# Gated feed-forward on one core: the second difference of the activations moved ahead of the first transient sum on VectorE, and the first difference's cast and lower part moved into the value's pass

## The chip, the cores and the metric

The kernel runs on one core of a Trainium2 chip. The metric is device time in microseconds (us) of one execution. Before the change three runs gave 2883.59, 2885.57 and 2885.86 us, so the median is 2885.57 us. The names of the engines are those of the profile: PE is TensorE (PEld its weight loads), DVE is VectorE, ACT is ScalarE, POOL is GpSimd, SP is SyncE, which here issues the DMAs.

## The reference

```python
# x is (8, 3008, 256); w_r, w_i are (256, 256); the feed-forward is 256 -> 1536 -> 256
X = np.fft.rfft(x, axis=1)
Yr = Xr @ w_r - Xi @ w_i + b_r
Yi = Xr @ w_i + Xi @ w_r + b_i
Yr = np.sign(Yr) * np.maximum(np.abs(Yr) - 0.01, 0.0)      # and Yi
y = np.fft.irfft(Y, n=3008, axis=1).reshape(24064, 256)
g = y @ w_gate
out = (g * (1 / (1 + np.exp(-g))) * (y @ w_val)) @ w_out
```

A Fourier layer with a soft threshold is followed by a gated feed-forward over 24064 tokens. Everything is float32.

## The kernel before

The kernel has two stages. `transform` does the Fourier layer, and in the trace it lasts about 680 us. `gated_ffn` does the rest, some 2200 us, and the change lies in it alone.

**Products.** A float32 operand is split into an upper part (its cast to fp32r) and a lower part (what the cast leaves). A product of two split operands is three matmuls that accumulate: weight-low times data-high, high times high, and high times low (`product`, L513, the matmul is on L516). Matrices are 2 by 2 blocks, and a 2 by 2 product is done with seven products in place of eight, by sums and differences of blocks.

**Blocks, pairs and halves.** The tokens come in 24 blocks. A block has two halves of 512 tokens (384 in the last two blocks), which are one side of the 2 by 2. Inside a block `q` runs over the six pairs of 128-wide slices of the hidden dimension (1536 = 6 x 2 x 128). Each `q` has two passes of `gate_or_value`: the gate (n = 0), which ends in a Silu, and the value (n = 1), which multiplies onto it. A pass has the seven up products of its weights, here called u1 to u7 (`up(bank, 1..7)`), in the order u1, u5, u6, u2, u7, u3, u4. Each product has its three matmuls.

**Down products.** While the gate and the value of one `q` are computed, the seven down products d1 to d7 of the pair before (`last`) are worked in between: d1, d3 and d2 in the gate, d6, d4, d7 and d5 in the value. So one `q` has 21 products, 63 matmuls, in this order on PE:

gate: u1, u5, d1, u6, d3, u2, u7, (inverse), u3, d2, u4; value: u1, u5, d6, u6, d4, u2, d7, u7, u3, d5, u4.

The piece "inverse" (L706) belongs to the last sequence of the Fourier layer: eight short matmuls in the gate of q = 2 of blocks 1 to 16.

**What d1 to d7 need.** The activations of a pair are four blocks H11, H12, H22 and H21 in `hidden`. VectorE makes four differences of them in `more` (`diff`, L527): T1 = H12 - H11, T3 = H22 - H12, T2 = H22 - T1, T4 = H21 - T2. Each of H11, H22, H21, T1, T3, T2, T4 is split: `upper` (L532) is the cast on ACT, `lower` (L536) the subtraction on POOL. d1 reads H11, d3 H22, d2 H21, d5 T1, d7 T3, d4 T4 and d6 T2. The differences all are done in the gate of the next pair, T1 and T3 at its start.

**PSUM.** There are eight banks. b1, b2 and b3 serve the up products. `spare` collects d1, then d1 + d6, then d1 + d6 + d7: after each, VectorE adds it to one of three running `sums` (`add`, L557, or a copy, L555, at q = 0), and must have read it before the next of the three writes it. Four banks hold totals over `q`. In each pass, ACT copies u1 from b1 to b3 (L623) and u5 from b2 to `m5` (L631); u6 is added onto b3 by PE, VectorE adds `m5` and b3 (L643), u7 is added onto b3, VectorE adds again (L666; in the gate the sum goes back to `m5`, which the Silu of H22 reads), then u4 is added onto b3. So u6 has to wait for the copy L623, u7 for the read on L643, and u4 for the read on L666.

**Order.** The four engines run in the order of the program, which is written out by hand (`tc.manual_schedule`); nothing reorders it. Besides the work above, ACT and POOL prepare the next block's `x` parts in the value passes: in q = 2 three sums on POOL (L502), in q = 3 one sum and two parts, in q = 4 two parts, in q = 5 three parts (a part is a cast on ACT, L510, and a subtraction on POOL, L511). When a block is complete, VectorE makes its outputs (`result`, L567) in the passes of the next block's q = 0 and q = 1.

Of the kernel before, what the change touches and what calls it, by code (L numbers as in the profile page):

```python
# [113 lines left out]
def f32(ap):  # L114
    return ap.bitcast(F32)
# [347 lines left out]
def gated_ffn(ctx, tc, front, ring, ps_, co, wdn, wup_d, xt_d, d2, out):  # L463

    nc = tc.nc
    v, g, act = nc.vector, nc.gpsimd, nc.scalar
# [9 lines left out]
    def load_unit(k):  # L476
        if k >= len(BLOCKS) * len(units):
            return
        held[k] = ring.tile([P, 2, 7, P], F32R, name="wup")
        nc.sync.dma_start(f32(held[k].rearrange("p i n a -> p i (n a)")), wup_d[units[k % len(units)]])  # L480
# [32 lines left out]
    def product(o, weights, parts, start, stop):  # L513

        for i, (w, x) in enumerate(((1, 0), (0, 0), (0, 1))):
            nc.tensor.matmul(o, lhsT=weights[w], rhs=parts[x], start=start and i == 0, stop=stop and i == 2, skip_group_check=True)  # L516


    H11, H12, H22, H21, T1, T3, T2, T4 = range(8)
    RIGHT = {1: H11, 3: H22, 2: H21, 5: T1, 7: T3, 4: T4, 6: T2}  # L520

    def at(i, h):
        return hidden[:, i, :h] if i < 4 else more[:, i - 4, :h]

    def diff(pair, o, a, b):
        h = pair["h"]
        v.tensor_tensor(at(o, h), at(a, h), at(b, h), op=ALU.subtract)  # L527

    def upper(pair, i):
        h = pair["h"]  # L530
        pair[i] = sbr.tile([P, 2, T], F32R, name="h_parts", bufs=8)
        act.copy(pair[i][:, 0, :h], at(i, h))  # L532

    def lower(eng, pair, i):
        h = pair["h"]
        eng.tensor_tensor(pair[i][:, 1, :h], at(i, h), f32(pair[i][:, 0, :h]), op=ALU.subtract)  # L536

    def down(pair, n_):

        h, q = pair["h"], pair["q"]  # L540
        weights = [part[:, q, A_AT[n_], :] for part in wdn]
        parts = [pair[RIGHT[n_]][:, x, :h] for x in range(2)]
        if n_ in total:
            product(total[n_][:, :h], weights, parts, q == 0, q == NQ - 1)
        else:
            product(spare[:, :h], weights, parts, n_ == 1, True)
# [4 lines left out]
    def add(pair, n_):  # L551
        h = pair["h"]
        o = sums[:, SUM_AT[n_], :h]
        if pair["q"] == 0:
            v.tensor_copy(o, spare[:, :h])  # L555
        else:
            v.tensor_tensor(o, o, spare[:, :h], op=ALU.add)  # L557

    def result(pair):

        h, blk = pair["h"], pair["blk"]
        o = {}

        def plus(c, j, n_, onto=None):
            if onto is not None:
                o[c, j] = sb.tile([P, T], F32, name="o", bufs=4)[:, :h]
            v.tensor_tensor(o[c, j], o[c, j] if onto is None else sums[:, onto, :h], total[n_][:, :h], op=ALU.add)  # L567

        def store(c, j):
            s = BLOCKS[blk][0] + (h if j == 1 else 0)  # L570
            nc.sync.dma_start(out[:, c - 1, s : s + h], o[c, j])

        plus(1, 1, 2, 0)
        store(1, 1)
        yield "after d2"
        plus(1, 2, 3, 1)
        yield "after d6"
        plus(2, 1, 4, 2)
        store(2, 1)
        yield "after d7"  # L580
        plus(1, 2, 5)
        store(1, 2)
        plus(2, 2, 5, 2)
        store(2, 2)
        yield "after d5"
# [3 lines left out]
    def step(name):  # L589

        if ends:
            assert next(ends["now"]) == name
            if name == "after d5":
                ends.clear()

    def gate_or_value(pair, last, n, k, extra):

        blk, q, h = pair["blk"], pair["q"], pair["h"]
        x = xs[blk]
        load_unit(k + RING - 1)  # L600
        m5 = hidden[:, 4 + n, :h]
        first = last is not None and last["q"] == 0
        closing = last is not None and last["q"] == NQ - 1

        def up(bank, n_, start):
            weights = [held[k][:, i, A_AT[n_], :] for i in range(2)]
            product(bank[:, :h], weights, [x[n_][:, i, :h] for i in range(2)], start, True)

        def done(after):
            for fn in extra.get(after, ()):  # L610
                fn()

        def take(i, src):

            if n == 0:
                act.activation(at(i, h), src, AF.Silu)  # L616
            else:
                v.tensor_tensor(at(i, h), at(i, h), src, op=ALU.mult)  # L618

        gate = n == 0 and last  # L620
        value = n == 1 and last
        up(b1, 1, True)
        act.copy(b3[:, :h], b1[:, :h])  # L623
        done(1)
        if gate:
            diff(last, T1, H12, H11)
            diff(last, T3, H22, H12)
        if value and first:
            step("after d5")
        up(b2, 5, True)  # L630
        act.copy(m5, b2[:, :h])  # L631
        done(5)
        if gate:
            upper(last, H21)
            lower(g, last, H21)
            upper(last, T3)
            lower(g, last, T3)
            down(last, 1)
        if value:
            down(last, 6)  # L640
            add(last, 6)
        up(b3, 6, False)
        v.tensor_tensor(b2[:, :h], m5, b3[:, :h], op=ALU.add)  # L643
        done(6)
        if gate:
            add(last, 1)
            down(last, 3)
            diff(last, T2, H22, T1)
        if value:
            if closing:  # L650
                step("after d6")
            down(last, 4)
        up(b1, 2, False)
        take(H11, b1[:, :h])
        if n:
            upper(pair, H11)
            lower(g, pair, H11)
        if gate:
            upper(last, T2)
            lower(g, last, T2)  # L660
        if value:
            down(last, 7)
            add(last, 7)
        up(b3, 7, False)
        last_sum = b1[:, :h] if n else m5
        v.tensor_tensor(last_sum, m5, b3[:, :h], op=ALU.add)  # L666
        if gate:
            diff(last, T4, H21, T2)
            if q == 2 and blk in pieces:
                inverse(pieces[blk])  # L670
        up(b2, 3, False)
        take(H22, last_sum)
        take(H12, b2[:, :h])
        if n:
            upper(pair, H22)
            lower(g, pair, H22)
        if gate:
            upper(last, T4)
            lower(g, last, T4)
            upper(last, T1)  # L680
            lower(g, last, T1)
            if first:
                step("after d7")
            down(last, 2)
            if closing:
                ends["now"] = result(last)
                step("after d2")
        if value:
            down(last, 5)
        up(b3, 4, False)  # L690
        take(H21, b3[:, :h])
# [11 lines left out]
    def inverse(u):  # L703
        for cc in range(2):
            for i in range(2):
                nc.tensor.matmul(  # L706
                    b1[:, cc * 188 + i * 94 : cc * 188 + (i + 1) * 94],
                    lhsT=part["z"][:, i * C + cc * P : i * C + (cc + 1) * P],
                    rhs=part["w"][:, i * 94 : (i + 1) * 94],
                    start=cc == 0 and i == 0,  # L710
                    stop=True,
                    skip_group_check=True,
                )
        xt = sbr.tile([P, 2, 188], F32, name="xt2")
        act.copy(xt.rearrange("p a b -> p (a b)"), b1[:, :376])
        nc.sync.dma_start(xt_d[B - 1][:, :, u * 188 : (u + 1) * 188], xt)
# [31 lines left out]
    last = None  # L748
    k = 0
    with tc.manual_schedule(engines={nc.tensor.engine, nc.vector.engine, nc.scalar.engine, nc.gpsimd.engine}):  # L750
        for blk, (_, h) in enumerate(BLOCKS):
            for q in range(NQ):
# [4 lines left out]
                last = pair  # L757
# [61 lines left out]
```

## Time and profile before

| | before |
|---|---|
| median of 3 runs | 2885.57 us |
| profiled execution, its time | 2883.66 us |
| its span, first to last instruction | 2881.9 us |
| mean granted TensorE clock | 0.990 |
| busy PE, PEld | 2734.9 us (95%), 2193.2 us (76%) |
| busy DVE, ACT, POOL | 2136.6 us (74%), 1721.8 us (60%), 1967.8 us (68%) |
| u and d matmuls (L516) | 9072 = 144 pairs x 63 |

In rows of the timeline the first number is the start in us from the span's start, the second how long the instructions of the row took, then engine, line, operation and tiles (written <- read), and how many instructions in a row were put together (x9). A bracket at the end gives the idle time of the engine ahead of the row and what ended it. A matmul's end is modelled and consecutive ones overlap, so the pace of PE is read from the starts.

### The profile page before, as it was taken

The numbers are of one execution on the slowest core, as the hardware profiler recorded it, in microseconds if no ns is written. First come the engines' busy times: TensorE is split into PE (matmuls) and PEld (weight loads), VectorE is DVE, ScalarE is ACT, GpSimd is POOL, SyncE is SP. The second block draws the span as 40 slices with busy tenths as digits, with TensorE's granted clock in tenths as the row PEclk, the third lists the DMA queues.
The fourth block names the chain that finished last, engine by engine and source line by source line (L and its number), as shares of the span: only waits on it lengthen the run. The fifth ranks groups of instructions, "written<-read, shape, count | busy, mean of one in ns | idle before, by whom it ended". The sixth has DMA issues, their size and how long they took to land. (4 is left out here: it accounts for less than half of the span.)

```text
span 2881.9 us, 39671 instructions
## 1 busy us (share of the span) xinstructions
PE 2734.9 (95%) x13173; PEld 2193.2 (76%) x13173; DVE 2136.6 (74%) x2916; ACT 1721.8 (60%) x3280; POOL 1967.8 (68%) x1574
## 2 busy tenths in 40 slices
PE   8989998899999999999999999999999999999998
PEld 5777787787777777777777777777777777777797
DVE  3766777875777777777777777777777777777777
ACT  5666666666565556556565556555565566555554
POOL 1555455564777778777777778777777777777775
PEclk9999999999999999999999999999999999999999
DMA  8788987664434444444434444444444443444442
GB/s 249 257 272 290 305 281 244 214 225 150 143 133 152 161 145 138 145 154 151 146 133 152 161 143 140 145 154 149 146 136 147 153 143 135 139 148 142 142 168 96
DMA packets 180124, 491.88 MB, mean 171 GB/s; under 512 B 17264, under 2 KB 89584, under 8 KB 179824
## 3 DMA queue, kind: packets, MB, share of 16 engines
q1 hardware_dynamic: 179920, 489.35, 51.4%
q8 instruction: 105, 1.72, 0.2%
q14 instruction: 99, 0.81, 0.1%
HBM read 378.65 MB, written 110.62 MB: 170 GB/s over the span
## 5 line engine op out<-in xcount | busy, mean ns | idle before, releaser
L516 PE MATMUL bank<-x_parts,wup 128*128 128x512 f32 (+1 forms) x6048 | 1551.3, 391 | 67.6 <-ACT bank L623 38.7
L516 PEld LDWEIGHTS bank<-x_parts,wup 128*128 128x128 f32 x6048 | 1108.9, 188 | 382.1 <-ACT bank L623 95.7
L536 POOL TENSOR_TENSOR h_parts<-more,h_parts 128x512 fp32r<-128x512 f32 (+1 forms) x573 | 769.5, 1354 | 191.1 <-ACT h_parts L532 185.9
L536 POOL TENSOR_TENSOR h_parts<-hidden,h_parts 128x512 fp32r<-128x512 f32 (+1 forms) x432 | 548.2, 1274 | 367.6 <-ACT h_parts L532 334.0
L516 PE MATMUL bank<-h_parts,wdn_hi 128*128 128x512 f32 (+1 forms) x2016 | 614.4, 386 | 0.9 <-POOL h_parts L536 0.9
L532 ACT CAST h_parts<-hidden 128x512 fp32r<-128x512 f32 (+1 forms) x432 | 264.9, 613 | 500.2 <-DVE hidden L618 500.2
L557 DVE TENSOR_TENSOR sums<-sums,bank 128x512 f32<-128x512 f32 (+1 forms) x360 | 242.7, 674 | 295.3 <-PE bank L516 295.3
L516 PEld LDWEIGHTS bank<-h_parts,wdn_hi 128*128 128x128 f32 x2016 | 378.2, 188 | 76.2 <-POOL h_parts L536 2.0
L618 DVE TENSOR_TENSOR hidden<-hidden,bank 128x512 f32<-128x512 f32 (+1 forms) x576 | 375.8, 674 | 79.8 <-PE bank L516 70.8
L532 ACT CAST h_parts<-more 128x512 fp32r<-128x512 f32 (+1 forms) x576 | 336.6, 610 | 158.3 <-DVE more L527 147.6
L516 PE MATMUL bank<-h_parts,wdn_lo 128*128 128x512 f32 (+1 forms) x1008 | 389.5, 386 | 4.2 <-DVE sums L557 4.2
L527 DVE TENSOR_TENSOR more<-hidden,more 128x512 f32<-128x512 f32 (+1 forms) x288 | 328.9, 1142 | 0.0
L616 ACT ACTIVATE hidden<-bank 128x512 f32<-128x512 f32 (+1 forms) x432 | 252.1, 584 | 126.0 <-PE bank L516 125.4
L643 DVE TENSOR_TENSOR bank<-hidden,bank 128x512 f32<-128x512 f32 (+1 forms) x288 | 197.3, 685 | 122.7 <-PE bank L516 91.5
L527 DVE TENSOR_TENSOR more<-hidden 128x512 f32<-128x512 f32 (+1 forms) x288 | 282.0, 1017 | 0.0
L623 ACT COPY bank<-bank 128x512 f32<-128x512 f32 (+1 forms) x288 | 161.6, 561 | 108.6 <-DVE hidden L618 103.9
L351 POOL TENSOR_TENSOR t<-t,y 128x512 f32<-128x512 f32 x96 | 132.9, 1384 | 136.2 <-DVE y L350 136.2
L516 PEld LDWEIGHTS bank<-h_parts,wdn_lo 128*128 128x128 f32 x1008 | 189.6, 188 | 41.7 <-issue 4.5
L511 POOL TENSOR_TENSOR x_parts<-xf,x_parts 128x512 fp32r<-128x512 f32 (+1 forms) x168 | 209.4, 1274 | 6.1 <-ACT x_parts L510 3.9
L316 POOL TENSOR_TENSOR f<-f 128x256 f32<-128x256 f32 x96 | 84.5, 880 | 149.1 <-ACT f L315 146.1
L631 ACT COPY hidden<-bank 128x512 f32<-128x512 f32 (+1 forms) x288 | 167.5, 582 | 1.8
L349 ACT COPY t<-mixb 64x256 f32<-64x256 f32 x384 | 140.6, 366 | 29.7 <-PE mixb L337 19.1
(94 smaller groups left out, 3278.3 us busy)
## 6 DMA issues: line engine op xcount, KB each, us to landing
wup<-wup_d SPq DMA_DIRECT2D x288, 896.0 KB, 4.6
d<-a SPq DMA_DIRECT2D x128, 192.0 KB, 4.3
a_in<-d SPq DMA_DIRECT2D x96, 256.0 KB, 4.4
out<-o SPq DMA_DIRECT2D x88, 256.0 KB, 6.4
scratch<-xp SPq DMA_DIRECT2D x116, 192.0 KB, 4.7
d<-z SPq DMA_DIRECT2D x84, 256.0 KB, 3.8
z_in<-d SPq DMA_DIRECT2D x56, 384.0 KB, 5.1
xt_d<-xt SPq DMA_DIRECT2D x56, 376.0 KB, 4.2
```

What stands on the lines that cost most here:

```text
L349: nc.scalar.copy(t[64 * half : 64 * half + 64, k * C : (k + 1) * C], mixb[64 * k : 64 * k + 64, half * C : (half + 1) * C])
L511: g.tensor_tensor(part[:, 1, :h], src, f32(part[:, 0, :h]), op=ALU.subtract)
L516: nc.tensor.matmul(o, lhsT=weights[w], rhs=parts[x], start=start and i == 0, stop=stop and i == 2, skip_group_check=True)
L527: v.tensor_tensor(at(o, h), at(a, h), at(b, h), op=ALU.subtract)
L532: act.copy(pair[i][:, 0, :h], at(i, h))
L536: eng.tensor_tensor(pair[i][:, 1, :h], at(i, h), f32(pair[i][:, 0, :h]), op=ALU.subtract)
L557: v.tensor_tensor(o, o, spare[:, :h], op=ALU.add)
L616: act.activation(at(i, h), src, AF.Silu)
L618: v.tensor_tensor(at(i, h), at(i, h), src, op=ALU.mult)
L623: act.copy(b3[:, :h], b1[:, :h])
L631: act.copy(m5, b2[:, :h])
L643: v.tensor_tensor(b2[:, :h], m5, b3[:, :h], op=ALU.add)
```

## The change

In the gate, VectorE's order behind L643 was: add of d1 (`add(last, 1)`), difference T2, L666, difference T4. It becomes: difference T2, L666, difference T4, add of d1. The cast of T1 on ACT and its lower part on POOL, which stood at the end of the gate behind those of T4, go to the value's pass, behind the copy of u5 (and behind the `x` parts that are placed after u1 and u5) and ahead of d6. Nothing is added or removed. The end of the program behind the last block is as before.

```diff
         if value:
+            upper(last, T1)
+            lower(g, last, T1)
             down(last, 6)
             add(last, 6)
         up(b3, 6, False)
         v.tensor_tensor(b2[:, :h], m5, b3[:, :h], op=ALU.add)
         done(6)
         if gate:
-            add(last, 1)
+            diff(last, T2, H22, T1)
             down(last, 3)
-            diff(last, T2, H22, T1)
...
         v.tensor_tensor(last_sum, m5, b3[:, :h], op=ALU.add)
         if gate:
             diff(last, T4, H21, T2)
+            add(last, 1)
             if q == 2 and blk in pieces:
                 inverse(pieces[blk])
...
         if gate:
             upper(last, T4)
             lower(g, last, T4)
-            upper(last, T1)
-            lower(g, last, T1)
             if first:
                 step("after d7")
```

## The prediction

> **What bounds the kernel now.** I read the stretch of the feed-forward first, in the view by windows (its columns are busy us and instructions of PE, PEld, DVE, ACT and POOL, then the granted clock, DMA share and GB/s), and then the row of the up matmuls in the view by lines.
>
> ```profile
> 681.00:2719.00 2038.00, 1976.10 (x8426) 1551.82 (x8426) 1556.93 (x2077) 1202.10 (x2151) 1526.22 (x1167) 1.00 0.43 145
> ```
>
> ```profile
> L516 PE MATMUL bank<-x_parts,wup 128*128 128x512 f32 (+1 forms) x6048 | 1551.3, 391 | 67.6 <-ACT bank L623 38.7 <-DVE hidden L666 28.4 <-POOL x_parts L511 0.2
> ```
>
> PE is busy 97% of the stretch at a granted clock of 1.00, no other engine over 77%. PE is the bound, and only what makes PE wait can pay. The row of the up matmuls names two causes beyond a trace of others: ACT's copy of u1 to b3 (L623) and VectorE's second sum (L666). The times there (38.7 and 28.4 us) are too small, since a matmul's end is modelled; the starts tell more. PE in q = 4 of block 12:
>
> ```profile
> 1857.74 2.20 PE L516 MATMUL bank<-x_parts,wup 128*128 128x512 f32 x9
> 1859.78 0.39 PE L516 MATMUL bank<-h_parts,wdn_lo 128*128 128x512 f32 x1
> 1860.00 0.61 PE L516 MATMUL bank<-h_parts,wdn_hi 128*128 128x512 f32 x2
> 1860.83 2.35 PE L516 MATMUL bank<-x_parts,wup 128*128 128x512 f32 x9 [0.21 <-DVE hidden L666]
> 1863.02 0.39 PE L516 MATMUL bank<-h_parts,wdn_lo 128*128 128x512 f32 x1
> 1863.25 0.61 PE L516 MATMUL bank<-h_parts,wdn_hi 128*128 128x512 f32 x2
> 1864.17 0.96 PE L516 MATMUL bank<-x_parts,wup 128*128 128x512 f32 x3 [0.30 <-ACT bank L623]
> 1864.97 0.40 PE L516 MATMUL bank<-h_parts,wdn_lo 128*128 128x512 f32 x1
> ```
>
> Nine matmuls without a wait take 1859.78 - 1857.74 = 2.04 us, so a matmul 0.227 and a product 0.68 us; the 63 of a pair would need 14.28 us. I count from d1 of this gate, three products ahead of the first row: 0 = 1855.70. Without waits the slots begin: u2 2.04, u7 2.72, u3 3.40, d2 4.08, u4 4.76, the value's u1 5.44, u5 6.12, d6 6.80, u6 7.48, d4 8.16, u2 8.84, d5 11.56, the next d1 14.28. The rows show two stalls, each with a refill behind it. d2 to u4 takes 1.05 in place of 0.68 and the nine from u4 2.19 in place of 2.04: 0.52. d6 to u6 takes 1.15 and u6 to d4 0.80, in place of 0.68 each: 0.59. Together 1.11 us a pair.
>
> In a pair with the inverse, d6 (1832.72) and u6 stand 0.68 apart, no wait:
>
> ```profile
> 1832.72 0.39 PE L516 MATMUL bank<-h_parts,wdn_lo 128*128 128x512 f32 x1
> ...
> 1833.40 0.90 PE L516 MATMUL bank<-x_parts,wup 128*128 128x512 f32 x3
> ```
>
> So 143 pairs with a pair before them less 16 with the inverse, 127 x 1.11 = 141 us, are there to be had.
>
> **The first stall, u4 waits for L666.** VectorE in the same pair:
>
> ```profile
> 1855.14 1.97 DVE L527 TENSOR_TENSOR more<-hidden 128x512 f32<-128x512 f32 x2
> 1857.33 0.70 DVE L643 TENSOR_TENSOR bank<-hidden,bank 128x512 f32<-128x512 f32 x1 [0.21 <-PE bank L516]
> 1857.93 0.68 DVE L557 TENSOR_TENSOR sums<-sums,bank 128x512 f32<-128x512 f32 x1
> 1858.53 1.65 DVE L527 TENSOR_TENSOR more<-hidden,more 128x512 f32<-128x512 f32 x1
> 1860.10 0.67 DVE L666 TENSOR_TENSOR hidden<-hidden,bank 128x512 f32<-128x512 f32 x1
> 1860.70 0.68 DVE L527 TENSOR_TENSOR more<-hidden,more 128x512 f32<-128x512 f32 x1
> ```
>
> L643 (at 1.63, 0.27 behind the end of u6's slot), add of d1, T2, L666 and T4 follow without a gap, so L666 (4.40 to 5.07) is late because VectorE is. T2 took 1.65 us, T4 0.68. The reason stands on POOL:
>
> ```profile
> 1849.66 1.30 POOL L502 TENSOR_TENSOR xf<-xf 128x512 f32<-128x512 f32 x1
> 1850.92 2.55 POOL L511 TENSOR_TENSOR x_parts<-xf,x_parts 128x512 fp32r<-128x512 f32 x2
> 1853.42 2.55 POOL L536 TENSOR_TENSOR h_parts<-hidden,h_parts 128x512 fp32r<-128x512 f32 x2
> 1857.08 1.30 POOL L536 TENSOR_TENSOR h_parts<-hidden,h_parts 128x512 fp32r<-128x512 f32 x1 [1.11 <-ACT h_parts L532]
> 1858.34 1.29 POOL L536 TENSOR_TENSOR h_parts<-more,h_parts 128x512 fp32r<-128x512 f32 x1
> 1860.91 4.20 POOL L536 TENSOR_TENSOR h_parts<-more,h_parts 128x512 fp32r<-128x512 f32 x3 [1.28 <-ACT h_parts L532]
> ```
>
> The lower part of H21 runs 1.38 to 2.68, that of T3 from 2.64 to 3.93; T2, issued within the latter, ended 0.55 behind it (4.48). T1 shows the same: issued under the lower part of H22. The Trainium skill, "SBUF — State Buffer", section "Who interferes with whom", says that a Vector instruction with two SBUF inputs contends with a GpSimd one that reads SBUF, and that the second issued blocks until the first is done; the 1.65 against 0.68 us agrees. That rule speaks against the change, which puts such an instruction where the add, with one input in PSUM, stood.
>
> Step 1: T2 issues where the add did, at 2.23, under the lower part of H21, with that of T3 queued behind. Who is served at 2.68? The end of block 21's last pair shows this very meeting, since there POOL was late:
>
> ```profile
> 2721.31 1.49 POOL L536 TENSOR_TENSOR h_parts<-hidden,h_parts 128x512 fp32r<-128x512 f32 x1 [0.82 <-ACT h_parts L532]
> 2722.75 1.75 POOL L536 TENSOR_TENSOR h_parts<-more,h_parts 128x512 fp32r<-128x512 f32 x1
> ```
>
> ```profile
> 2722.62 0.72 DVE L527 TENSOR_TENSOR more<-hidden,more 128x512 f32<-128x512 f32 x1
> ```
>
> T2 was issued under the lower part of H21 (to 2722.80) and ended at 2723.34, 0.54 behind it; the next lower part took 1.75 us in place of 1.29. VectorE goes first. So T2 ends at 3.23 (it ended at 4.48), the lower part of T3 runs 2.64 to 4.39.
>
> Step 2: u7's slot ends at 3.40; with the 0.27 of L643 its result is there at 3.67. L666 is now held by PE: 3.67 to 4.34, and u4, due at 4.76, doesn't wait. The stall of 0.52 goes, with 0.42 to spare.
>
> Step 3: T4 issues at 4.27, waits for T3's lower part (4.39) and ends at 4.94. The lower part of T2 then ends at 4.39 + 1.75 = 6.1; d6 reads it in its third matmul, at 7.25. Hidden.
>
> Step 4: the add of d1 comes last, 4.86 to 5.54. d6 overwrites `spare` at 6.80: 1.26 us of cover. In q = 0 and 1 one to three output sums (L567) queue behind it on VectorE, 0.6 us each, then the add of d6, whose input comes at 7.75. Were the cover gone, d6 would wait for as much as is lacking.
>
> **The second stall, u6 waits for ACT's copy.** ACT in the same pair: cast T2, Silu H22 (of `m5`), Silu H12, casts T4 and T1, Silu H21, L623, L631:
>
> ```profile
> 1860.21 0.62 ACT L532 CAST h_parts<-more 128x512 fp32r<-128x512 f32 x1 [0.94 <-DVE more L527]
> 1860.87 0.63 ACT L616 ACTIVATE hidden<-hidden 128x512 f32<-128x512 f32 x1
> 1861.40 0.58 ACT L616 ACTIVATE hidden<-bank 128x512 f32<-128x512 f32 x1
> 1861.88 1.13 ACT L532 CAST h_parts<-more 128x512 fp32r<-128x512 f32 x2
> 1862.91 0.60 ACT L616 ACTIVATE hidden<-bank 128x512 f32<-128x512 f32 x1
> 1863.54 0.57 ACT L623 COPY bank<-bank 128x512 f32<-128x512 f32 x1
> 1864.02 0.59 ACT L631 COPY hidden<-bank 128x512 f32<-128x512 f32 x1
> ```
>
> The Silu of H22 starts 0.10 behind L666, and from its start to u6's (1864.17) it is 3.30 us of ACT without a gap. One cast in there is T1's: half of 1862.91 - 1861.88, 0.51. Without it 2.79.
>
> Step 5: Silu H22 starts at 4.44, so u6 is free at 4.44 + 2.79 = 7.23, ahead of its slot at 7.48. The T4 cast at 5.45 finds T4 done (4.94), Silu H21 at 5.97 finds u4 done (5.44 + 0.27). The stall of 0.59 goes too, with only 0.25 to spare.
>
> Step 6: T1's cast is now behind L623 and L631 (to 7.67) on ACT, so 7.56 to 8.18; ahead of the cast of H11 ACT has room (that waits for u2, 9.5). On POOL the lower part of T1 runs 8.26 to 9.56, after an idle 0.9 us behind that of T4. It ended at 9.41 before (1860.91 + 4.20). d5 reads it at 12.0: hidden. In q = 5 it stands behind two `x` parts, to 11.55: still hidden. No DMA is moved.
>
> **What is late next.** Behind T1 on POOL stand the `x` work and the lower parts of H11 and H22, and the pair is now 1.11 us shorter. In the pair ahead of the rows (q = 3) POOL's last piece, the lower part of H22, began at 1854.66 or -1.04; the one of H11 ended there. New: 9.56, one sum and two parts (1.26 + 2.50), H11 1.25, so H11's ends at 14.57, and the next d1 is at 14.28: +0.29. Now T1, issued at -0.56, waits until 0.29 and ends at 0.84. T3 follows on VectorE, H22's lower part on POOL. Who is next there?
>
> ```profile
> 463.11 0.69 DVE L355 TENSOR_TENSOR y_lo<-t,y_hi 128x512 fp32r<-128x512 f32 x1 [0.26 <-ACT y_hi L354]
> 463.72 1.48 DVE L319 TENSOR_TENSOR f_lo<-f,f_hi 128x768 fp32r<-128x768 f32 x1
> ```
>
> ```profile
> 463.12 1.26 POOL L316 TENSOR_TENSOR f<-f 128x256 f32<-128x256 f32 x1
> ```
>
> POOL's instruction, blocked by L355 from 463.11 to 463.80, came between the two of VectorE: L319 ended at 465.20, 0.82 behind it. They take turns. So H22's lower part (1.75) ends at 2.0, T3 at 2.55, L643 runs 2.47 to 3.17, and u7, due at 2.72, starts at 3.23: a new stall of 0.51 in the gate of q = 4. For q = 3, behind three sums (3.9 us), the same working gives an end at +0.40 and a stall of 0.62, or a stall of 0.40 in the 16 blocks where the inverse makes the pair longer. For the gate behind q = 5 H11's lower part ends at -0.2: none. Per run 22 x 0.51 + 16 x 0.40 + 6 x 0.62 = 21 us. The bounds are 0 (POOL catches up) and 1.1 for three gates a block, 73 us.
>
> **Sum.** 141 - 21 = 120 us off. The profiled execution took 2883.66 us (span 2881.9); it would take 2764. It stands 1.9 us under the median of 2885.57, so 2766. The last two blocks, of 384 tokens, are taken at the same price, an estimate.
>
> **Rivals.**
> (a) No new stall: the lower parts are never late enough. For it: the idle POOL times before H21's lower part (1.11 us in the rows). Against it: 5.0 us of POOL work behind T1 in q = 3. 2885.6 - 141 = 2745.
> (b) POOL falls behind further, and three gates a block stall 1.1 us each: 2885.6 - 141 + 73 = 2818. For it: POOL is busy 75% and the pairs become shorter. Against it: the pairs of q = 0, 1 and 4 have 1.3 to 3.8 us less of its work.
> (c) POOL keeps the port over both lower parts, so T2 ends at 4.48 as before, L666 too, and u4's stall stays. Then Silu H22 is at 5.17 as before, u6 free at 7.96 for a slot at 7.48 + 0.52 = 8.00, and only the second stall goes: 127 x 0.59 = 75, 2811. The skill's rule quoted above leaves this open, as it tells of two instructions and not of a third queued. Against it stands block 21's row.
> (d) Slower: POOL's queue behind the later T1 turns over to the next gates. The new stall is 0.22 more than the end of H11's lower part counted from d1 (0.51 for 0.29). It decides where three gates in 22 blocks lose 141 + 6 us, 2.2 each, that is from an end at +2.0, 1.7 us later than I work out. At +2.4 it is 66 x 2.62 = 173 us, 2918. Nothing in the rows lasts that much longer.
> (e) The change doesn't do what it says: L666 is held by something else than VectorE's queue, and ACT's chain by another wait than its length. Then about 2886. Against it: neither engine's rows have a gap.
>
> **How the numbers follow.** About 0.2%, 6 us, is what a measurement of this kernel can tell from no change. Forecast 0.68, (a) 0.12, (b) 0.08, (c) 0.06, (d) 0.03, (e) 0.03. Faster is all but (d) and (e), 0.94. The range takes in (a) at its low end, and leaves out (b) to (e), 0.20 in all: from 2744, up to 2806, where the late gates cost about three times what I reckon (61 us).
>
> **What will show it.** Right: L666 begins about 3.7 behind d1 with a gap ahead of it that PE ends; T2 takes about 1.0; T3's lower part about 1.75; the up matmuls' idle time names L666 and L623 hardly at all; pairs of q = 1 and q = 5 take about 14.3 us; u7 is late in the gates of q = 3 and q = 4 alone, with L643 as the one it waits for. Step 1 is wrong if T2 still ends 0.55 behind T3's lower part; step 4 if d6 waits for L557; step 5 if u6 still waits for L623, where my margin is least (0.25); the part on what is late next if u7 stalls in more gates or in none.

## The result, and the profile after

| | before | after |
|---|---|---|
| median | 2884.58 us (4 runs) | 2767.8 us (4 runs, 2764.52 to 2773.95) |
| profiled execution | 2883.66 us, span 2881.9 | 2764.52 us, span 2762.6 |
| granted clock | 0.990 | 0.991 |

The ratio of the times is 0.9597, 95% interval 0.958 to 0.9615: 4.0% faster.

The first view is again that by windows, over the same 22 blocks as the stretch shown in the prediction (681 to 2719 us there, here 676.6 to 2610.4), then the view by lines for the up matmuls, their weight loads and those of the down products' upper weights. In the changed kernel L645 is the first sum on VectorE (L643 before), L667 the second (L666 before).

```profile
676.60:2610.40 1933.80, 1930.34 (x8424) 1559.61 (x8423) 1577.52 (x2077) 1199.42 (x2150) 1649.83 (x1167) 1.00 0.45 153
```

```profile
L516 PE MATMUL bank<-x_parts,wup 128*128 128x512 f32 (+1 forms) x6048 | 1530.6, 387 | 1.2 <-POOL x_parts L511 0.7 <-ACT bank L623 0.2 <-DVE bank L645 0.2
L516 PEld LDWEIGHTS bank<-x_parts,wup 128*128 128x128 f32 x6048 | 1122.6, 188 | 239.2 <-DVE bank L645 22.3 <-POOL x_parts L511 3.3 <-ACT bank L623 2.0
L516 PEld LDWEIGHTS bank<-h_parts,wdn_hi 128*128 128x128 f32 x2016 | 378.1, 188 | 97.3 <-POOL h_parts L536 26.3
```

The 22 blocks take 1934 us in place of 2038. PE is busy 99.8% of it (97% before) at a granted clock of 1.00. The idle time that the up matmuls showed before, 67.6 us, is 1.2. Neither the copy of u1 (L623) nor the second sum holds PE any more. The weight loads show two new waits: for the first sum (L645), 22.3 us, and for POOL's lower parts (L536), 26.3 us where it was 2.0 before.

Part of the gain in this one execution is not the change's. The feed-forward's first up matmul, ahead of which nothing was changed, came 4.6 us earlier:

```profile
681.18 1.05 PE L516 MATMUL bank<-x_parts,wup 128*128 128x512 f32 x2
```

```profile
676.61 1.05 PE L516 MATMUL bank<-x_parts,wup 128*128 128x512 f32 x2
```

So of the 119.3 us between the two spans, 114.7 lie in the feed-forward. Four runs of one kernel differ by up to 10 us, and the first up matmul began between 676.6 and 685.5 us in the traces of this study, so the traces' matmul starts tell a few us better than the times do.

**A pair without POOL work for the next block** (gate of q = 1, block 12; d1 began at 1750.58, three products ahead of the first row). PE:

```profile
1752.62 2.20 PE L516 MATMUL bank<-x_parts,wup 128*128 128x512 f32 x9
1754.66 0.39 PE L516 MATMUL bank<-h_parts,wdn_lo 128*128 128x512 f32 x1
1754.89 0.61 PE L516 MATMUL bank<-h_parts,wdn_hi 128*128 128x512 f32 x2
1755.34 2.20 PE L516 MATMUL bank<-x_parts,wup 128*128 128x512 f32 x9
1757.38 0.39 PE L516 MATMUL bank<-h_parts,wdn_lo 128*128 128x512 f32 x1
1757.61 0.61 PE L516 MATMUL bank<-h_parts,wdn_hi 128*128 128x512 f32 x2
1758.06 0.84 PE L516 MATMUL bank<-x_parts,wup 128*128 128x512 f32 x3
1758.74 0.39 PE L516 MATMUL bank<-h_parts,wdn_lo 128*128 128x512 f32 x1
```

d2 to u4 takes 0.68, the nine matmuls from u4 2.04, d6 to u6 0.68, u6 to d4 0.68. Both stalls are gone, refills included; the next d1 stands in the trace at 1764.86, 14.28 us behind this one. VectorE and POOL in the same gate:

```profile
1752.21 0.70 DVE L645 TENSOR_TENSOR bank<-hidden,bank 128x512 f32<-128x512 f32 x1 [0.24 <-PE bank L516]
1752.82 1.00 DVE L527 TENSOR_TENSOR more<-hidden,more 128x512 f32<-128x512 f32 x1
1754.18 0.69 DVE L667 TENSOR_TENSOR hidden<-hidden,bank 128x512 f32<-128x512 f32 x1 [0.36 <-PE bank L516]
1754.79 0.73 DVE L527 TENSOR_TENSOR more<-hidden,more 128x512 f32<-128x512 f32 x1
1755.44 0.68 DVE L555 COPY sums<-bank 128x512 f32<-128x512 f32 x1
```

```profile
1751.97 1.30 POOL L536 TENSOR_TENSOR h_parts<-hidden,h_parts 128x512 fp32r<-128x512 f32 x1 [1.15 <-DVE more L527]
1753.22 4.74 POOL L536 TENSOR_TENSOR h_parts<-more,h_parts 128x512 fp32r<-128x512 f32 x3
1758.79 1.29 POOL L536 TENSOR_TENSOR h_parts<-more,h_parts 128x512 fp32r<-128x512 f32 x1 [0.82 <-ACT h_parts L532]
```

T2 is issued at 1752.82 under the lower part of H21 (1751.97 to 1753.27) and ends at 1753.82, 0.55 behind it, while the lower part of T3 is queued on POOL. L667 then starts with a gap that PE ended: 3.60 behind d1. ACT, from the Silu of H22 to the copy of u5 and T1's cast:

```profile
1754.96 0.63 ACT L616 ACTIVATE hidden<-hidden 128x512 f32<-128x512 f32 x1 [0.30 <-POOL h_parts L536]
1755.50 0.58 ACT L616 ACTIVATE hidden<-bank 128x512 f32<-128x512 f32 x1
1755.98 0.61 ACT L532 CAST h_parts<-more 128x512 fp32r<-128x512 f32 x1
1756.48 0.60 ACT L616 ACTIVATE hidden<-bank 128x512 f32<-128x512 f32 x1
1757.12 0.57 ACT L623 COPY bank<-bank 128x512 f32<-128x512 f32 x1
1757.60 0.60 ACT L631 COPY hidden<-bank 128x512 f32<-128x512 f32 x1
1758.08 0.63 ACT L532 CAST h_parts<-more 128x512 fp32r<-128x512 f32 x1
```

The bracket ahead of the first Silu names POOL, but in this gate T3's lower part and the second sum end at about the same time; in the late gate below the Silu starts before T3's lower part has ended, and in both 0.09 behind the second sum, which is what it waits for. It starts at 4.38 behind d1, the copy that u6 waits for (1757.12) ends at 7.11, and u6 starts at its slot, 7.48.

**A late gate** (q = 4 of the same block, behind the pair with one sum and two parts on POOL; d1 is the first row). PE, VectorE, POOL:

```profile
1795.45 0.39 PE L516 MATMUL bank<-h_parts,wdn_lo 128*128 128x512 f32 x1
...
1797.07 0.86 PE L516 MATMUL bank<-h_parts,wdn_hi 128*128 128x512 f32 x2
1797.76 2.47 PE L516 MATMUL bank<-x_parts,wup 128*128 128x512 f32 x9
1800.07 0.39 PE L516 MATMUL bank<-h_parts,wdn_lo 128*128 128x512 f32 x1
```

```profile
1794.89 3.03 DVE L527 TENSOR_TENSOR more<-hidden 128x512 f32<-128x512 f32 x2
1797.84 0.68 DVE L645 TENSOR_TENSOR bank<-hidden,bank 128x512 f32<-128x512 f32 x1
1798.44 1.18 DVE L527 TENSOR_TENSOR more<-hidden,more 128x512 f32<-128x512 f32 x1
1799.58 0.69 DVE L667 TENSOR_TENSOR hidden<-hidden,bank 128x512 f32<-128x512 f32 x1
```

```profile
1790.60 1.30 POOL L502 TENSOR_TENSOR xf<-xf 128x512 f32<-128x512 f32 x1
1791.86 2.55 POOL L511 TENSOR_TENSOR x_parts<-xf,x_parts 128x512 fp32r<-128x512 f32 x2
1794.37 4.71 POOL L536 TENSOR_TENSOR h_parts<-hidden,h_parts 128x512 fp32r<-128x512 f32 x3
```

POOL did the sum and the two parts, then three lower parts in one go, 4.71 us for what takes 3.9 alone: that of H11 ends 0.22 behind d1 (1794.37 + 1.30). T1 and T3 on VectorE take 3.03 us together. L645 follows at 2.39 behind d1, and PE waits twice: in the last matmul of d3, which reads the lower part of H22 (u2 comes 0.69 behind 1797.07, where 0.45 would do), and at u7, inside the row of nine, 2.31 us in place of 2.04.

### The profile page after: what moved, and what is told of

The parts are those of the page before. It is cut to its first block, busy times and chain, and to the rows that moved or that the text cites. A ratio compares the mean times of both kernels' runs of the same rounds, so it can differ in the third digit from the quotient of the medians.

```text
span 2762.6 us, 39633 instructions
## 1 busy us (share of the span) xinstructions
PE 2684.7 (97%) x13173; PEld 2200.4 (80%) x13173; DVE 2157.9 (78%) x2916; ACT 1718.8 (62%) x3280; POOL 2096.8 (76%) x1574
## 5 line engine op out<-in xcount | busy, mean ns | idle before, releaser
L516 PE MATMUL bank<-x_parts,wup 128*128 128x512 f32 (+1 forms) x6048 | 1530.6, 387 | 1.2 <-POOL x_parts L511 0.7
L516 PEld LDWEIGHTS bank<-x_parts,wup 128*128 128x128 f32 x6048 | 1122.6, 188 | 239.2 <-DVE bank L645 22.3
L536 POOL TENSOR_TENSOR h_parts<-more,h_parts 128x512 fp32r<-128x512 f32 (+1 forms) x573 | 846.3, 1492 | 97.8 <-ACT h_parts L532 84.2
L536 POOL TENSOR_TENSOR h_parts<-hidden,h_parts 128x512 fp32r<-128x512 f32 (+1 forms) x432 | 602.9, 1408 | 210.1 <-ACT h_parts L532 167.3
L516 PE MATMUL bank<-h_parts,wdn_hi 128*128 128x512 f32 (+1 forms) x2016 | 627.2, 389 | 2.1 <-POOL h_parts L536 0.9
L516 PEld LDWEIGHTS bank<-h_parts,wdn_hi 128*128 128x128 f32 x2016 | 378.1, 188 | 97.3 <-POOL h_parts L536 26.3
L532 ACT CAST h_parts<-more 128x512 fp32r<-128x512 f32 (+1 forms) x576 | 351.7, 611 | 103.6 <-DVE more L527 94.9
L527 DVE TENSOR_TENSOR more<-hidden 128x512 f32<-128x512 f32 (+1 forms) x288 | 341.0, 1222 | 0.0
L527 DVE TENSOR_TENSOR more<-hidden,more 128x512 f32<-128x512 f32 (+1 forms) x288 | 284.5, 988 | 0.0
L623 ACT COPY bank<-bank 128x512 f32<-128x512 f32 (+1 forms) x288 | 161.6, 561 | 109.4 <-DVE hidden L618 104.0
L645 DVE TENSOR_TENSOR bank<-hidden,bank 128x512 f32<-128x512 f32 (+1 forms) x288 | 196.3, 681 | 37.2 <-PE bank L516 27.4
```

## The experiments

The theory: PE had two stalls a pair with a cause each. u4's came from VectorE, where T2 stood behind the add and so was issued under the second of two lower parts in a row on POOL, and waited for its end; u6's came from ACT's chain, too long by T1's cast. The new, smaller waits come from POOL's queue in the gates behind a pair with `x` work. (The port in the expectations is what such a VectorE instruction and POOL wait for each other about.) Rival 1: T1's move is the one lever. Rival 2: what held the second sum was the add's own 0.7 us on VectorE. Rival 3: the new waits are VectorE being full, whatever POOL does.

All runs in one table. The columns give by how many us a pair exceeds the 14.28 us of its 63 matmuls, from the starts of PE's matmuls, mean of blocks 2 to 15; in q = 2 the place of the inverse is left out. The times are medians. In the expectations, e3 is the kernel "changed, add behind T2" and e4 "changed, two sums ahead of T1".

| kernel | us | q = 0 | 1 | 2 | 3 | 4 | 5 |
|---|---|---|---|---|---|---|---|
| before | 2884.6 | 1.11 | 1.12 | 0.11 | 1.15 | 1.12 | 1.12 |
| changed | 2767.8 | 0.09 | 0 | 0.02 | 0.65 | 0.56 | 0 |
| changed, again | 2771.6 | 0.10 | 0 | 0.02 | 0.64 | 0.57 | 0 |
| VectorE's order alone | 2786.4 | 0.33 | 0.33 | 0.02 | 0.33 | 0.33 | 0.33 |
| T1's move alone | 2824.2 | 0.27 | 0.61 | 0.04 | 0.80 | 0.80 | 0.61 |
| changed, add behind T2 | 2806.8 | 0.64 | 0.02 | 0.03 | 0.99 | 1.08 | 0.01 |
| changed, two sums ahead of T1 | 2736.7 | 0.09 | 0 | 0.01 | 0 | 0 | 0 |
| changed, one sum ahead of T1 | 2757.4 | 0.10 | 0 | 0.02 | 0 | 0.58 | 0 |
| changed, T1 behind u1's copy | 2748.4 | 0.10 | 0 | 0.02 | 0.05 | 0.09 | 0 |
| two sums ahead, add behind T2 | 2768.2 | 0.60 | 0.03 | 0.03 | 0.02 | 0.36 | 0.01 |
| two sums ahead, inverse behind u3 | 2735.8 | 0.08 | 0 | 0.04 | 0 | 0 | 0 |

**VectorE's order alone.** The kernel before, with

```diff
-            add(last, 1)
+            diff(last, T2, H22, T1)
             down(last, 3)
-            diff(last, T2, H22, T1)
...
             diff(last, T4, H21, T2)
+            add(last, 1)
```

> Theory (two stalls, two causes): the new order on VectorE alone (T2 behind L643, the add of d1 last; T1 stays in the gate) takes u4's stall of 0.52 away. Silu H22 starts at 4.44 behind d1, ACT's chain with T1's cast in it is 3.30, so u6 is free at 7.74 for a slot at 7.48: 0.26 of the second stall and its refill of 0.12 stay. 127 x 0.73 = 93 us off, 2792 (2780 to 2800). POOL does T1's lower part right behind that of T4, so no new stall in the gates of q = 3 and 4. Rival 1 (T1's move is the one lever, VectorE's order does little): above 2860. Rival 2 (what held L666 was the add's 0.7 us of VectorE and not where T2 meets POOL): the same time as the theory, so this run alone does not tell it apart.

Measured 2786.37 us, ratio 0.9657 (0.9642 to 0.9671). 0.33 us a pair stay, where 0.38 were worked out, and all at u6. The weight loads of this kernel in the view by lines:

```profile
L516 PEld LDWEIGHTS bank<-x_parts,wup 128*128 128x128 f32 x6048 | 1119.7, 188 | 272.6 <-ACT bank L623 61.4 <-POOL x_parts L511 1.9 <-DVE bank L643 0.9
```

L623 is the one that counts. There are no late gates, since POOL does T1's lower part right behind T4's. Rival 1 falls: the order alone gives 99 of the 117 us.

**T1's move alone.** The kernel before, with

```diff
         if value:
+            upper(last, T1)
+            lower(g, last, T1)
             down(last, 6)
...
-            upper(last, T1)
-            lower(g, last, T1)
             if first:
```

> Theory: only the cast and the lower part of T1 go to the value's pass, VectorE's order is that of before. L666 stays at 4.40 and u4's stall of 0.52 stays. Silu H22 at 5.17 and a chain of 2.79 free u6 at 7.96 for a slot at 8.00: the stall of 0.59 goes, 75 us off. T1's lower part ends on POOL at about 10.3 with a pair of 14.80 us, so the lower part of H11 ends at about +0.5 in the gates of q = 3 and q = 4: some 0.7 us of new stall in 44 gates, 30 us back. 2840, or 2810 without the new stalls. Rival 1 (T1's move is the one lever): 2768, as with the whole change.

Measured 2824.15 us, ratio 0.9793 (0.9777 to 0.981), between the two values that were given. In q = 1 and q = 5 the 0.52 at u4 stays (0.49 here, refill included), and 0.06 at u6. In q = 3 and q = 4 the new wait of 0.65 at d3 and u7 appears, but there u4 then waits only 0.13: PE is already later, so the two waits overlap, which the expectation added up. The weight loads name all three releasers (L645 is the first sum in this kernel, L668 the second):

```profile
L516 PEld LDWEIGHTS bank<-x_parts,wup 128*128 128x128 f32 x6048 | 1113.3, 188 | 296.2 <-DVE hidden L668 46.8 <-DVE bank L645 26.0 <-ACT bank L623 16.3
```

The two parts' gains, 99 and 61 us, are together more than the 117 of the whole, for two reasons that the table shows: in a plain pair either edit frees u6 sooner (0.79 and 0.51 of 1.12, together 1.30), and T1's move brings the late gates along.

**The add's place.** The changed kernel, with

```diff
             diff(last, T2, H22, T1)
+            add(last, 1)
             down(last, 3)
...
             diff(last, T4, H21, T2)
-            add(last, 1)
```

> The changed kernel with the add of d1 right behind T2, so ahead of L666. Theory: T2 ends at 3.23, the add runs 3.15 to 3.83, L666 3.75 to 4.42 in place of 3.67 to 4.34. The 0.08 is inside the margins of 0.42 (u4) and 0.25 (u6): the time of the changed kernel, 2768, within 6 us. Rival 2 (the add ahead of L666 is what held it): u4's stall of 0.52 comes back, 66 us, 2834.

Measured 2806.82 us, ratio 0.9729 (0.9714 to 0.9743): 39 us slower than the changed kernel, so the expectation was missed, and rival 2's 2834 as well. The columns tell why: 0.02 and 0.01 in q = 1 and q = 5, as the theory has it, but 0.34, 0.52 and 0.55 more in q = 3, 4 and 0, 31 us over 22 blocks; the starts of the last two blocks give 7 more. VectorE in the gate of q = 3 of block 12 (d1 at 1803.81):

```profile
1806.40 0.68 DVE L645 TENSOR_TENSOR bank<-hidden,bank 128x512 f32<-128x512 f32 x1
1807.00 1.18 DVE L527 TENSOR_TENSOR more<-hidden,more 128x512 f32<-128x512 f32 x1
1808.10 0.68 DVE L557 TENSOR_TENSOR sums<-sums,bank 128x512 f32<-128x512 f32 x1
1808.70 0.67 DVE L668 TENSOR_TENSOR hidden<-hidden,bank 128x512 f32<-128x512 f32 x1
```

T2 ends at 1808.18, 4.4 behind d1 and about when u7's result is there in this gate, so that the add's 0.6 us goes straight onto the second sum (1808.70 to 1809.37). u4, due at 1809.31, begins at 1809.42, with a refill behind it. The margins that the expectation counted with are those of a gate that POOL does not hold up. In such gates (q = 1 and q = 5) rival 2 falls: the add stands ahead of the second sum there, and costs 0.01 to 0.02 us as long as T2 goes first. Putting the add last is worth nothing in two gates of six and 39 us in all.

**POOL's queue.** Two sums for the next block go ahead of T1's lower part, into the time in which POOL waits for T1's cast:

```diff
-        for i, (q, n) in enumerate(((2, 1), (2, 1), (2, 1), (3, 1))):
-            later(ahead, q, n, 6, lambda blk=blk, i=i: x_sum(blk, *SUMS[i]))
+        for i, (q, n, at_) in enumerate(((2, 1, 1), (2, 1, 6), (2, 1, 6), (3, 1, 1))):
+            later(ahead, q, n, at_, lambda blk=blk, i=i: x_sum(blk, *SUMS[i]))
```

The changed kernel ran again on the same chip as this one, the kernel with T1 between the copies and the one with the add's place again.

> The changed kernel as it is, on the chip of the next three, to compare with them: 2768, within 6 us.

Measured 2771.59 us (2767.14 to 2774.68).

> The changed kernel with two of the four sums of x (the first in q = 2 and the one in q = 3) placed behind u1's copy of the value's pass, so ahead of T1's lower part on POOL, where POOL waits 0.5 to 1.4 us for T1's cast. Theory (the new stalls in the gates of q = 3 and q = 4 come from POOL's queue: H11's lower part ends at +0.2 to +0.4 behind d1, T1, H22's lower part and T3 take turns on the port, and L643 and the third matmul of d3 are late): H11's lower part ends about 0.9 us sooner, 0.65 + 0.56 us a block go, 20 blocks: 24 us less than the changed kernel, 2744. Rival 3 (VectorE is just full at the shorter pair, POOL's queue is not the cause): 2768.

Measured 2736.67 us, ratio to before 0.9491 (0.9477 to 0.9504), 35 us under the changed kernel beside it, where 24 were expected; the matmul starts account for 1.2 us a block, 27 us over 22 blocks. The rest is no more than runs of one kernel differ by. POOL in q = 2 of this kernel (T4's lower part, a sum, T1's, two sums, those of H11 and H22) and the view by windows:

```profile
1852.78 1.29 POOL L536 TENSOR_TENSOR h_parts<-more,h_parts 128x512 fp32r<-128x512 f32 x1 [0.80 <-ACT h_parts L532]
1854.03 1.30 POOL L502 TENSOR_TENSOR xf<-xf 128x512 f32<-128x512 f32 x1
1855.34 1.29 POOL L536 TENSOR_TENSOR h_parts<-more,h_parts 128x512 fp32r<-128x512 f32 x1
1856.58 2.54 POOL L502 TENSOR_TENSOR xf<-xf 128x512 f32<-128x512 f32 x2
1859.09 2.60 POOL L536 TENSOR_TENSOR h_parts<-hidden,h_parts 128x512 fp32r<-128x512 f32 x2
```

```profile
700.00:1600.00 900.00, 899.32 (x3992) 741.23 (x3992) 721.37 (x983) 562.51 (x1012) 761.91 (x549) 1.00 0.46 156
```

The sum fills the wait, and the gates of q = 3 and q = 4 are not late any more. Rival 3 falls: VectorE has the same work, and PE is busy 899.3 of 900 us. This version beats both kernels.

With the first sum of q = 2 alone placed so, `(3, 1, 6)` in place of `(3, 1, 1)`:

> As e4, but only the first sum of q = 2 goes ahead of T1's lower part; the sum of q = 3 stays where it was. Theory (each late gate comes from the POOL queue of the pair right ahead of it): the gate of q = 3 has no stall, that of q = 4 keeps its 0.56: some 13 us above e4, as much below the changed kernel, 2750 to 2756. If the lateness were carried on from one gate to the next, q = 4 would be free as well: the time of e4, 2737.

Measured 2757.38 us (2752.08 to 2759.04), ratio 0.9555 (0.9542 to 0.9568). The time is 1 us over the expected 2750 to 2756. By the starts, q = 3 is free and q = 4 keeps its 0.58: each late gate comes from the queue of the pair ahead of it and is not carried on.

**T1 between the copies.** The changed kernel, with T1's cast and lower part behind the copy of u1:

```diff
         act.copy(b3[:, :h], b1[:, :h])
+        if value:
+            upper(last, T1)
+            lower(g, last, T1)
         done(1)
...
         if value:
-            upper(last, T1)
-            lower(g, last, T1)
             down(last, 6)
```

> The changed kernel with T1's cast and lower part ahead of the copy of u5, right behind the copy of u1 that u6 waits for. ACT's chain to u6 stays 2.79, so no second stall; T1's lower part begins about 0.5 us sooner. Theory: H11's lower part ends at -0.3 in the gates of q = 4 (stall gone) and at about -0.1 in those of q = 3 (0.1 left), about 1.1 us a block: 22 us less than the changed kernel, 2746. Rival 3: 2768. Were the copy of u5, now 0.5 later, to hold L643 of the value's pass and then u7, some 0.1 us in 143 pairs would be lost: 2782.

Measured 2748.39 us (2740.46 to 2748.86), ratio 0.9517 (0.9504 to 0.953). 0.05 and 0.09 are left in q = 3 and q = 4. Half a microsecond sooner on POOL is enough, and the later copy of u5 costs nothing.

**The add's place again**, in the kernel with the two sums ahead:

> e4 with the add of d1 right behind T2, ahead of L666. In e3 that place of the add cost 39 us, all of it in the gates of q = 3, q = 4 and q = 0, where POOL was late, and nothing in q = 1 and q = 5. Theory: the add costs only where POOL's queue has used up VectorE's margin; with POOL on time in q = 3 and q = 4 it costs at most 0.6 us in the gate of q = 0: within 12 us of e4. Rival 2 (the add ahead of L666 holds it by itself): 39 us above e4 here too.

Measured 2768.22 us, ratio 0.9598 (0.9585 to 0.9611): 31 us above the kernel with the add last, not 12. It is half a hit. q = 3 is free (0.02), as the theory has it; q = 0 has its 0.60; but q = 4 loses 0.36. VectorE in the gate of q = 4 of the kernel with the add last shows how little room there is:

```profile
1877.39 0.68 DVE L645 TENSOR_TENSOR bank<-hidden,bank 128x512 f32<-128x512 f32 x1
1877.99 1.19 DVE L527 TENSOR_TENSOR more<-hidden,more 128x512 f32<-128x512 f32 x1
1879.32 0.69 DVE L667 TENSOR_TENSOR hidden<-hidden,bank 128x512 f32<-128x512 f32 x1
```

Ahead of the second sum (1879.32) lies a gap of 0.14, against 0.36 in the gate of q = 1. The add's 0.60 makes it 0.46 late, more than the 0.42 to spare at u4 and the 0.25 at u6. The columns give 0.95 us a block, 21 us over 22 blocks, and the starts of the last two blocks 6 more. The other 4 are less than runs of one kernel differ by.

**The inverse behind u3.** The last place in the blocks where PE waits regularly:

```diff
-            if q == 2 and blk in pieces:
-                inverse(pieces[blk])
         up(b2, 3, False)
         take(H22, last_sum)
         take(H12, b2[:, :h])
+        if gate and q == 2 and blk in pieces:
+            inverse(pieces[blk])
```

> e4 with the inverse's eight matmuls and its copy behind u3 in place of ahead of it. In e4 the only wait of PE left in the blocks is that of the inverse for the Silu of H11 (0.63, with 0.09 behind it, in 16 gates). Behind u3 that Silu is long done, and the copy of b1 is read ahead of the value's u1: 16 x 0.7 = 11 us less than e4, 2726. If ACT, which now does the copy between Silu H12 and T4's cast, frees u6 too late, up to 0.5 us in 16 gates comes back: 2734.

Measured 2735.83 us (2732.63 to 2738.31), ratio 0.9483 (0.947 to 0.9496): 1 us from the kernel without this edit, and measured apart from it, so no gain that the times can tell. PE in this kernel, then in the one without the edit:

```profile
1838.71 1.03 PE L706 MATMUL bank<-w,z 96*128 96x94 f32 x8
1839.52 0.47 PE L516 MATMUL bank<-h_parts,wdn_lo 128*128 128x512 f32 x1
```

```profile
1847.94 1.52 PE L516 MATMUL bank<-x_parts,wup 128*128 128x512 f32 x6
1849.53 1.13 PE L706 MATMUL bank<-w,z 96*128 96x94 f32 x8
1850.45 0.71 PE L516 MATMUL bank<-x_parts,wup 128*128 128x512 f32 x2
```

With nothing to wait for, the eight matmuls take 0.81 us; ahead of u3 they took 0.92 with a wait of 0.23 before (1847.94 + 6 x 0.227 = 1849.30). The wait was real but a third of what I took for it: the rest was the matmuls' own pace, 0.10 us each. 0.3 us in 16 gates is 5 us.

## Why the prediction came out

The forecast was 2766 us and the time 2767.8. That it is so close is in part luck: the feed-forward gained 114.7 us and not 120, and in the profiled execution (2764 forecast, 2764.52 measured) the first stage, which the change does not touch, gave 4.6 us more. By its steps:

- **Steps 1 and 2** (T2 ends at 3.23, L666 at 3.67, u4 on time). T2 ended at 3.24 behind d1 and the second sum began at 3.60. Right in mechanism and size; the run with the order alone has no wait at u4.
- **Steps 3 and 4** (T4 and the add last, both covered). In q = 1 the add, there a copy, starts at 4.86, as worked out, and d6 does not wait. The prediction didn't ask what the add would have cost between T2 and the second sum: 39 us, by the late gates.
- **Step 5** (Silu H22 at 4.44, u6 free at 7.23). 4.38 and 7.11, with u6 on its slot. The run with the order alone, with T1's cast back in the chain, has 0.33 at u6 where 0.38 follows from the working.
- **Step 6 and what is late next.** T1's lower part began 8.21 behind d1 (8.26 worked out), POOL having waited 0.82. In the gate of q = 4 H11's lower part ended at 0.22 (0.29), the first sum, now L645, began at 2.39 (2.47), and the pair lost 0.56 (0.51). But the prediction put all of it at u7, while in the rows 0.24 came earlier, at d3, whose third matmul reads the lower part of H22. Its own numbers had this: that matmul was due at 1.36 + 0.45 = 1.81, and the lower part was to end at 2.0. The size was hardly touched, since u7 waits for L645 in either case. That VectorE and POOL take turns, which rested on one row of the first stage, shows in T1 and T3's 3.03 us.
- **Terms that were mis-sized.** The gate of q = 3 behind the inverse lost 0.65 in place of 0.40: in the pair ahead, the inverse makes PE 1.25 us longer, but T1's lower part also begins 1.24 later (9.44 behind d1 in most of these gates, against 8.20 in blocks 17 and 20, without the inverse). The working left that delay out. The inverse's copy on ACT (L715) stands ahead of the Silu of H22 there, but it does not set the delay: behind it ACT still waits for PE, 0.16 us ahead of the Silu of H21 (0.45 in block 12), since u4 comes later by the inverse. Without the inverse, in blocks 17 to 20, the gate lost 0.67 to 0.86 (0.62). And q = 0 lost 0.09 in place of nothing. With 16 x 0.25, 22 x 0.05 and 22 x 0.09 the sum of 120 us becomes 113; the feed-forward gained 114.7. The last two blocks, taken at the same price, gave 10.8 us of it for their 12 pairs.
- **The rivals.** (a), no new stall, is what the kernel with two sums ahead of T1 reaches in the blocks. (b) and (d) fall with the late gates as small as reckoned. (c), POOL keeping the port, falls with T2's end. (e) falls with the two parts, each of which removed its own wait.

Shown by a run: the two causes, each alone; POOL's queue as the source of the late gates; the cost of the add between T2 and the second sum. Only read from traces: that VectorE's subtractions wait for POOL's instructions and not for something else, and that the turns of the two make up the 3.03 us. Taking the contention away altogether was not tried.

## What to carry to other kernels

When one engine is the bound, count its work at its unhindered pace from starts, not ends: 63 matmuls of 0.227 us against a pair of 15.4 gave the size of the gain, where the idle times showed half of it. Then write the chain to each wait with its start, end and margin for a plain iteration, and again for the iterations in which another engine has extra work, because margins that hold in the first are used up in the second (the add's place: nothing or 0.5 us, by the gate). An engine that is moved to wait for something new has room there for work that is due later: one sum put into POOL's wait took away a stall on PE.

## What the runs showed of the hardware that was not expected

A VectorE subtraction of two SBUF operands (128x512) that meets a POOL instruction with another queued behind is served between the two: T2 took 1.00 us in the plain gate, 0.55 of it behind the lower part of H21, and POOL's next took 1.74 to 1.75 us in place of 1.29. The second sum, which has one operand in PSUM, took 0.69 us under the same lower part of T3. Two such instructions of VectorE in a row don't keep POOL out; it comes in between (T1 and T3 with 3.03 us). The prediction had this from single rows, and it held in the gates shown. The Trainium skill, "SBUF — State Buffer", section "Who interferes with whom", has the second issued block until the first is done, which the rows bear out: T2 ends behind the lower part under which it was issued. With a third instruction queued, the two engines took turns here. The eight short matmuls of the inverse (96*128, 96x94 in the rows) go at 0.10 us each with nothing to wait for, so eight of them take as long as 3.6 matmuls of 512 columns (0.227 us each).
